# Decoding attention on one Trainium2 core: K and V of two sequences in one transfer each, and outputs gathered into token rows

## The chip, the cores and the metric

The kernel runs on one core of a Trainium2 chip. The metric is the device time of one execution in microseconds (us), the median of three runs. Engines are named as in the profile: PE multiplies matrices (PEld loads its weights), DVE, ACT and POOL work on vectors, SP here only issues DMAs. Sixteen DMA engines move data between HBM and the on-chip memory SBUF; PE writes its sums into the accumulator memory PSUM.

## What is computed

Eight sequences (B) bring four new tokens each (Sq). There are 32 query heads and 8 heads of K and V, so four query heads (rep) share one K and V; each head has 128 elements and the cache 2048 positions. All data are bf16.

```python
q = (x @ wq).reshape(B, Sq, Hq, Dh).transpose(0, 2, 1, 3)
k = jnp.repeat(k_cache, rep, axis=1)
v = jnp.repeat(v_cache, rep, axis=1)
scores = jnp.einsum("bhqd,bhkd->bhqk", q, k) * (Dh ** -0.5)
p = softmax(scores, axis=-1)
o = jnp.einsum("bhqk,bhkd->bhqd", p, v)
out = o.transpose(0, 2, 1, 3).reshape(B, Sq, Hq * Dh) @ wo
```

K and V are 33.5 MB each, wq and wo 4.2 MB each, x 32 KB: 75.5 MB in all, read once.

## The kernel before

The work is cut into eight units (NU). Unit u is a group of four K/V heads (G) and a pair of sequences (NB = 2); units 0 to 3 have the first group (gg = 0), units 4 to 7 the second. The 128 partitions hold four heads times 32 stretches of 64 positions (C), so one sequence's K of a unit is 2 MiB, 16 KB in a row on each partition.

**Loads.** All loads are issued on SP's queue into `ring`, eight slots of 2 MiB (L65, L67). `loads` (L118 to L123) lists them in order: K of unit 0, first sequence; x; wq in two halves; K of unit 0, second sequence; K of unit 1; then V of unit u and K of unit u + 2 in turn; last V in four pieces of 1 MiB (`load_last_v`) and wo (`load_wo`), its first half (for gg = 0) in rows of 4 KB, its second half in five pieces. `issue(done)` (L125) issues as many as the ring has slots for, once before the units and once at the end of each unit's pass (L368); a load into a slot that is still read waits on SP, and the loads behind it with it.

**One pass of the unit loop (L341).** For each of four tiles t of 16 positions: `turn` transposes the tile of K on DVE, once for either sequence (kt, six buffers); `scores` multiplies it with the queries on PE, eight matmuls into `s_ps`. In unit 7 the turns of the first sequence stand, like those of all units but 0, each ahead of the second's. `top` takes the maxima on DVE in two halves, `exps` the exponentials on ACT with their sums, `weights` transposes the result on DVE (pt) and copies it into `p_bd`, four block rows for each half h: three on ACT, one on POOL. `norm` makes the reciprocal of the sums on DVE. Then, one unit behind, `values(u-1)` multiplies with V on PE, 32 matmuls for each half, and `scaled` multiplies the result with the reciprocal on ACT into `o_sb`.

**Outputs.** The result of a unit has rows (head, sequence, query head, token), and a row computed both sequences' V; only the column block of its own sequence counts. Two units behind, `by_heads` (L280) gathers the right blocks by two matmuls with a permutation `perm`, and `to_rows` (L287) copies them (o_r) and transposes them on DVE into `oP`, once per unit. `project` (L298) multiplies `oP` with wo on PE into `out_ps`, 64 matmuls of 256 columns in all, after the last unit's values. The order at the end (L369 to L376): half of the first group's projection, `by_heads` and `to_rows` of unit 7, the other half, and the second group's projection as the pieces of wo land. Then one copy on ACT and two DMAs out.

The order on each engine is the order of the calls (`manual_schedule`, L63); waits between engines come from the data.

Of the kernel before, what the change touches and what calls it, by code (L numbers as in the profile page):

```python
# [17 lines left out]
def kernel(  # L18
# [31 lines left out]
    DH = D // 2  # L50
    scale = float(Dh) ** -0.5
# [19 lines left out]
    perm = const.tile([128, NB, 128], BF16, name="perm")  # L71
# [4 lines left out]
    oP = [const.tile([128, G, 4, NP, NB * Sq], BF16, name=f"oP{i}") for i in range(NG)]  # L76
# [11 lines left out]
    def load_kv(kind, u, b):  # L88
        gg, bp = units[u]
        src = (k_cache if kind == "k" else v_cache)[NB * bp + b, G * gg : G * gg + G]  # L90
        nc.sync.dma_start(  # L91
            ring[:, take((kind, u, b)), :], src.rearrange("g (s c) d -> (g s) (c d)", c=C)
        )

    def load_last_v(u):
        gg, bp = units[u]
        slots = [take(("v", u, b)) for b in range(NB)]
        for h in range(2):
            for b in range(NB):
                src = v_cache[NB * bp + b, G * gg : G * gg + G]  # L100
                nc.sync.dma_start(
                    ring[:, slots[b], h * CH * Dh : (h + 1) * CH * Dh],
                    src.rearrange("g (s c) d -> (g s) (c d)", c=C)[:, h * CH * Dh : (h + 1) * CH * Dh],
                )

    def load_wq(h):
        rows = wq.rearrange("(p r) n -> p (r n)", r=R)
        n = C * Dh
        nc.sync.dma_start(ring[:, take(("wq", h)), :], rows[:, h * n : (h + 1) * n])  # L109

    def load_wo(gg, cuts):
        slot = take(("wo", gg))
        rows = wo[gg * G * 512 : (gg + 1) * G * 512, :].rearrange("(k p r) j -> p k (r j)", k=G, r=4)
        to = ring[:, slot, :].rearrange("p (k n) -> p k n", k=G)
        for g0, g1, r0, r1 in cuts:
            nc.sync.dma_start(to[:, g0:g1, r0 * D : r1 * D], rows[:, g0:g1, r0 * D : r1 * D])

    loads = [("k", 0, 0), ("x",), ("wq", 0), ("wq", 1), ("k", 0, 1), ("k", 1, 0), ("k", 1, 1)]  # L118
    for u in range(NU):
        if u + 2 < NU:  # L120
            loads += [("v", u, 0), ("v", u, 1), ("k", u + 2, 0), ("k", u + 2, 1)]
    loads += [("v", NU - 2, 0), ("v", NU - 2, 1), ("vlast", NU - 1), ("wo", 0), ("wo", 1)]
    loads.reverse()  # L123

    def issue(done):  # L125

        while loads:
            what = loads[-1]
            if what[0] != "x" and n_loads[0] + (what[0] == "vlast") >= done + NS:
                return  # L130
            loads.pop()
            if what[0] in "kv":
                load_kv(*what)
            elif what[0] == "x":
                nc.sync.dma_start(x_sb[:, :], x.flatten_outer_dims())  # L135
            elif what[0] == "wq":
                load_wq(what[1])
            elif what[0] == "vlast":
                load_last_v(what[1])
            elif what[1] == 0:  # L140
                load_wo(0, [(0, 4, 0, 4)])
            else:
                load_wo(1, [(0, 1, 0, 4), (1, 2, 0, 4), (2, 3, 0, 4), (3, 4, 0, 2), (3, 4, 2, 4)])

    issue(0)
# [7 lines left out]
    by_row = ident[:, :].rearrange("k (g b r s) -> k b r g s", g=G, b=NB, r=rep)  # L153
    for b in range(NB):
        nc.gpsimd.tensor_copy(
            out=perm[:, b, :].rearrange("k (r g b s) -> k b r g s", r=rep, g=G, b=NB)[:, b],
            in_=by_row[:, b],
        )
# [3 lines left out]
    def turn(u, b, t):  # L162

        kt = ktpool.tile([128, CT, J, S, 2], BF16, tag="kt", name="kt")
        n = CT * Dh
        nc.vector.transpose(  # L166
            out=kt[:, :, :, :, :].rearrange("w c j s e -> w (c j s e)").bitcast(FP32),
            in_=ring[:, slot_of["k", u, b], t * n : (t + 1) * n].bitcast(FP32),
        )
        kts[u, b, t] = kt  # L170
# [28 lines left out]
    def top(u, h):  # L199
        if h == 0:  # L200
            stats[u] = [small.tile([128, n], FP32, tag=f"stat{i}", name=f"stat{i}") for i, n in enumerate((2, 1, 2, 1))]
        nc.vector.tensor_reduce(  # L202
            out=stats[u][0][:, h : h + 1],
            in_=s_ps[:, 2 * h : 2 * h + 2, :].rearrange("q t n -> q (t n)"),
            axis=AX,
            op=ALU.max,
            negate=True,
        )
# [26 lines left out]
    def weights(u, h):  # L235
        pt = small.tile([128, CH // 2, 32, 2], BF16, tag="pt", name="pt")
        nc.vector.transpose(  # L237
            out=pt[:, :, :, :].rearrange("s c q e -> s (c q e)").bitcast(FP32),
            in_=ps[u, h][:, :, :, :].rearrange("q c s e -> q (c s e)").bitcast(FP32),
        )  # L240
        pb = pbs[u, h] = p_bd[(2 * u + h) % 4]
        for g in range(G):
            rows = slice(g * 32, (g + 1) * 32)
            copy = nc.gpsimd.tensor_copy if g == G - 1 else nc.scalar.copy
            copy(out=pb[rows, :, g, :, :], in_=pt[rows, :, :, :])  # L245

    def norm(u):
        nc.vector.tensor_tensor(
            out=stats[u][3][:, :], in0=stats[u][2][:, 0:1], in1=stats[u][2][:, 1:2], op=ALU.add
        )  # L250
        nc.vector.reciprocal(stats[u][3][:, :], stats[u][3][:, :])
# [3 lines left out]
    def values(u, h):  # L255
        if h == 0:
            o_pss[u] = psum_o.tile([128, NB, Dh], FP32, tag="o", name="o_ps")
        a, b = (slot_of["v", u, i] for i in range(NB))
        v = (ring[:, a : b + 1 : b - a, :] if b > a else ring[:, a : (b - 1 if b else None) : b - a, :])
        v = v.rearrange("p b (c d) -> p b c d", d=Dh)  # L260
        for i in range(CH):
            nc.tensor.matmul(  # L262
                o_pss[u][:, :, :],
                lhsT=pbs[u, h][:, i // 2, :, :, i % 2].rearrange("s g q -> s (g q)"),
                rhs=v[:, :, h * CH + i, :],
                start=(h == 0 and i == 0),
                stop=(h == 1 and i == CH - 1),
            )
# [11 lines left out]
    def by_heads(u):  # L280
        o_pm = o_pms[u] = psum_m.tile([128, Dh], FP32, tag="m", name="o_pm")
        for b in range(NB):
            nc.tensor.matmul(  # L283
                o_pm[:, :], lhsT=perm[:, b, :], rhs=o_sbs[u][:, b, :], start=(b == 0), stop=(b == NB - 1)
            )

    def to_rows(u):  # L287
        gg, bp = units[u]
        o_r = small.tile([128, 4, 32], BF16, tag="o_r", name="o_r")
        nc.vector.tensor_copy(  # L290
            out=o_r[:, :, :], in_=o_pms[u][:, :].rearrange("q (d r) -> q r d", r=4)
        )
        nc.vector.transpose(
            out=oP[gg][:, :, :, bp, :].rearrange("d g r t -> d r g t"),
            in_=o_r[:, :, :].rearrange("q r d -> q (r d)"),
        )

    def project(gg, g, r0, n):  # L298
        w = ring[:, slot_of["wo", gg], :].rearrange("p (k r j) -> p k r j", k=G, r=4)
        for r in range(r0, r0 + n):  # L300
            for half in range(2):
                nc.tensor.matmul(  # L302
                    out_ps[half * T : (half + 1) * T, :],
                    lhsT=oP[gg][:, g, r, :, :].rearrange("d p t -> d (p t)"),
                    rhs=w[:, g, r, half * DH : (half + 1) * DH],
                    start=(gg == 0 and g == 0 and r == 0),
                    stop=(gg == NG - 1 and g == G - 1 and r == 3),
# [10 lines left out]
    for gg in range(NG):  # L318
        psq = psum_o.tile([128, rep * Dh], FP32, tag="o", name="psq")
        for r in range(R):  # L320
            w = ring[:, slot_of["wq", r // 2], :].rearrange("p (r n) -> p r n", r=2)[:, r % 2, :]
# [19 lines left out]
    for u in range(NU + 1):  # L341
        if u < NU:
            for t in range(NT):
# [3 lines left out]
                scores(u, t)  # L347
            if u >= 2:
                by_heads(u - 2)
# [4 lines left out]
            if u >= 2:  # L354
                to_rows(u - 2)
# [5 lines left out]
        if u >= 1:  # L361
            values(u - 1, 0)
            if u == NU:
                by_heads(u - 2)
                to_rows(u - 2)
# [46 lines left out]
```

## Time and profile before

| | us |
|---|---|
| runs (median of 3) | 186.34 (186.31 to 186.52) |
| the profiled execution | 186.44 |
| its span, first to last instruction | 184.3 |
| PE busy | 136.6 (74%) |
| DVE busy | 117.3 (64%) |
| ACT busy | 78.2 (42%) |
| POOL busy | 36.2 (20%) |

The mean granted PE clock is 0.953. The core read 75.53 MB from HBM. Busy shares are means over the whole span; which engine sets the end is read from the chain of waits, which follows back from the last instruction what released each step. A row of the timeline gives start, duration, engine, line, operation, output<-inputs, count, and in brackets the idle time before it with what ended it. A row of a windows view gives, behind the window and its length, busy time and count of PE, PEld, DVE, ACT and POOL, then the granted clock, the share of the DMA engines and GB/s. A DMA summary row gives packets, bytes and the rate in its window.

### The profile page before, as it was taken

How to read it: one execution, taken by the hardware profiler on the slowest of the kernel's cores; microseconds unless marked ns; L12 is line 12 of the kernel's file. 1: busy time of each engine (PE TensorE's matmuls, PEld its weight loads, DVE VectorE, ACT ScalarE, POOL GpSimd, SP SyncE). 2: the span in 40 equal slices, each digit the busy share in tenths (PEclk: the TensorE clock that was granted, in tenths of full speed). 3: DMA queues.
4: the chain of work that ended last, by engine and by line, in shares of the span. 5: the costliest groups of instructions: out<-in, count | busy, mean ns of one | idle time of the engine just before them, and what ended most of it. 6: DMA issues, size and time to landing. Idle time of an engine off the chain costs nothing.

```text
span 184.3 us, 2298 instructions
## 1 busy us (share of the span) xinstructions
PE 136.6 (74%) x884; PEld 81.5 (44%) x884; DVE 117.3 (64%) x147; ACT 78.2 (42%) x93; POOL 36.2 (20%) x92
## 2 busy tenths in 40 slices
PE   0001799039997998989759994989498949997992
PEld 0000233013683376338523771368135823486880
DVE  6680290689649976977488666976497549661110
ACT  2000200494079219905950298019900891059410
POOL 8500420080025005200800061005200210003000
PEclk9999999957999999999987999999979996999999
DMA  5999999999999999999999999999999999999980
GB/s 192 430 430 434 437 423 437 427 430 430 427 437 430 425 434 420 439 430 430 427 427 434 427 443 427 423 430 427 444 427 430 430 420 441 414 430 409 421 344 11
DMA packets 6586, 75.71 MB, mean 411 GB/s; under 512 B 720, under 2 KB 816, under 8 KB 1968
## 3 DMA queue, kind: packets, MB, share of 16 engines
q1 hardware_dynamic: 6528, 75.55, 96.6%
q8 instruction: 7, 0.11, 0.2%
q10 hardware_dynamic: 48, 0.02, 0.0%
q14 instruction: 3, 0.02, 0.0%
HBM read 75.53 MB, written 0.03 MB: 410 GB/s over the span
## 4 chain that ended last, share of the span: by engine, by line
DMA 68%; DVE 12%; PE 9%; issue 4%; ACT 3%; POOL 1%; SPq 1%; ACTq 0%; DVEq 0%; POOLq 0%
DMA ring<-in_k_cache_dram 43%; DMA ring<-in_v_cache_dram 17%; PE s_ps L189 9%; DVE kt L166 8%; DMA ring<-in_wo_dram 8%; DVE stat L202 3%; ACT p_sb L223 2%; POOL p_bd L245 1%; DVE pt L237 1%; SPq L109 1%; DVE stat L210 0%; SPq L135 0%; PE out_ps L302 0%; SPq L91 0%; ACT out_sb L379 0%
## 5 line engine op out<-in xcount | busy, mean ns | idle before, releaser
L189 PE MATMUL s_ps<-kt,q_bd 128*128 128x512 bf16 x256 | 70.5, 420 | 23.9 <-DVE kt L166 10.3
L166 DVE STREAM_TRANSPOSE kt<-ring 128x1024 f32<-128x1024 f32 x64 | 73.5, 1210 | 11.9 <-DMA ring<-in_k_cache_dram 11.9
L262 PE MATMUL o_ps<-ring,p_bd 128*128 128x256 bf16 x512 | 57.3, 272 | 3.2 <-DMA ring<-in_v_cache_dram 2.0
L189 PEld LDWEIGHTS <-q_bd 128*128 128x128 bf16 x256 | 25.9, 103 | 67.5 <-issue 31.6
L262 PEld LDWEIGHTS <-p_bd 128*128 128x128 bf16 x512 | 49.8, 98 | 9.9 <-issue 4.1
L223 ACT ACTIVATE p_sb<-s_ps,stat 128x1024 bf16<-128x1024 f32 x16 | 22.0, 1402 | 75.5 <-DVE stat L210 75.5
L245 ACT COPY p_bd<-pt 32x1024 bf16<-32x1024 bf16 x48 | 49.9, 1040 | 0.5
L245 POOL COPY p_bd<-pt 32x1024 bf16<-32x1024 bf16 x16 | 16.6, 1038 | 115.7 <-DVE pt L237 113.2
L202 DVE TENSOR_REDUCE stat<-s_ps 128x1 f32<-128x1024 f32 x16 | 18.9, 1220 | 13.3 <-PE s_ps L189 13.3
L237 DVE STREAM_TRANSPOSE pt<-p_sb 128x512 f32<-128x512 f32 x16 | 11.4, 711 | 15.0 <-ACT p_sb L223 15.0
L178 POOL COPY q_bd<-qT 32x64 bf16<-32x64 bf16 x64 | 13.0, 229 | 15.4 <-DVE qT L334 13.6
L323 PE MATMUL psq<-ring,xT_sb 128*32 128x512 bf16 x32 | 3.8, 626 | 8.2 <-DMA ring<-in_wq_dram 8.2
L290 DVE CAST o_r<-o_pm 128x128 bf16<-128x128 f32 x8 | 2.3, 284 | 10.1 <-PE o_pm L283 10.1
L314 PE MATMUL xtp<-ident,x_sb 32*128 32x32 bf16 x4 | 0.3, 192 | 8.9 <-DMA x_sb<-in_x_dram 8.9
L149 DVE MEMSET p_bd<- 128x2048 uint32 x3 | 5.3, 1765 | 2.0 <-PEq L396 1.2
L334 DVE STREAM_TRANSPOSE qT<-q_sb 128x64 f32<-128x64 f32 x8 | 1.2, 212 | 7.9 <-ACT q_sb L330 7.9
L330 ACT CAST q_sb<-psq 128x512 bf16<-128x512 f32 x2 | 1.2, 585 | 11.2 <-PE psq L323 11.2
L323 PEld LDWEIGHTS <-xT_sb 128*32 128x32 bf16 x32 | 1.2, 129 | 10.0 <-issue 9.5
L274 ACT ACTIVATE o_sb<-o_ps,stat 128x256 bf16<-128x256 f32 x8 | 3.8, 474 | 4.1 <-issue 3.9
L302 PE MATMUL out_ps<-ring,oP 128*32 128x256 bf16 x64 | 4.1, 273 | 0.2 <-DMA ring<-in_wo_dram 0.2
L314 PEld LDWEIGHTS <-x_sb 32*128 32x128 bf16 x4 | 0.2, 114 | 8.9 <-DMA x_sb<-in_x_dram 8.9
L302 PEld LDWEIGHTS <-oP 128*32 128x32 bf16 x64 | 3.0, 96 | 1.1 <-issue 0.6
(20 smaller groups left out, 21.9 us busy)
## 6 DMA issues: line engine op xcount, KB each, us to landing
ring<-in_k_cache_dram SPq DMA_DIRECT2D x16, 2048.0 KB, 27.1
ring<-in_v_cache_dram SPq DMA_DIRECT2D x14, 2048.0 KB, 30.1
ring<-in_wq_dram SPq DMA_DIRECT2D x2, 2048.0 KB, 14.1
ring<-in_v_cache_dram SPq DMA_DIRECT2D x4, 1024.0 KB, 29.4
ring<-in_wo_dram SPq DMA_DIRECT2D x1, 2048.0 KB, 26.9
ring<-in_wo_dram SPq DMA_DIRECT2D x3, 512.0 KB, 22.1
ring<-in_wo_dram SPq DMA_DIRECT2D x2, 256.0 KB, 15.7
x_sb<-in_x_dram SPq DMA_DIRECT2D x1, 32.0 KB, 7.7
```

Source lines behind the costliest of these rows:

```text
L149: nc.vector.memset(t[:, :, :, :, :], 0.0)
L166: nc.vector.transpose(out=kt[:, :, :, :, :].rearrange("w c j s e -> w (c j s e)").bitcast(FP32), in_=ring[:, slot_of["k", u, b], t * n : ( ...
L178: nc.gpsimd.tensor_copy(out=qb[rows, b, :, g, b, :].rearrange("w (j e) q -> w j e q", e=2), in_=qT[rows, gg, :, NB * bp + b, :, :, :].rear ...
L189: nc.tensor.matmul(s_ps[:, t, :], lhsT=q_bd[u % 2][:, b, 2 * j + e, :, :, :].rearrange("w g b q -> w (g b q)"), rhs=kts[u, b, t][:, :, j, ...
L202: nc.vector.tensor_reduce(out=stats[u][0][:, h : h + 1], in_=s_ps[:, 2 * h : 2 * h + 2, :].rearrange("q t n -> q (t n)"), axis=AX, op=ALU.max,
L223: nc.scalar.activation(out=p_sb[:, :, :, :].rearrange("q c s e -> q c e s"), in_=s_ps[:, 2 * h : 2 * h + 2, :].rearrange("q t (c e s) -> q ...
L237: nc.vector.transpose(out=pt[:, :, :, :].rearrange("s c q e -> s (c q e)").bitcast(FP32), in_=ps[u, h][:, :, :, :].rearrange("q c s e -> q ...
L245: copy(out=pb[rows, :, g, :, :], in_=pt[rows, :, :, :])
L262: nc.tensor.matmul(o_pss[u][:, :, :], lhsT=pbs[u, h][:, i // 2, :, :, i % 2].rearrange("s g q -> s (g q)"), rhs=v[:, :, h * CH + i, :], st ...
L274: nc.scalar.activation(out=o_sb[:, :, :], in_=o_pss[u][:, :, :], func=COPY, scale=stats[u][3][:, :])
L302: nc.tensor.matmul(out_ps[half * T : (half + 1) * T, :], lhsT=oP[gg][:, g, r, :, :].rearrange("d p t -> d (p t)"), rhs=w[:, g, r, half * D ...
L323: nc.tensor.matmul(psq[g * T : (g + 1) * T, :], lhsT=xT_sb[:, r, :], rhs=w[:, (gg * G + g) * rep * Dh : (gg * G + g + 1) * rep * Dh], star ...
```

## The change

- **Ring and loads.** Four slots of 4 MiB instead of eight of 2 MiB. K of a unit is one transfer for both sequences, and so is V; a partition gets two rows of 16 KB, which lie 4 MiB apart in HBM. K of unit 0 stays in two transfers, with x between them and the whole of wq (one transfer) ahead of the second. The last V comes in two halves of positions, each for both sequences. `issue` is called with 2 + 2u.
- **wo.** A partition holds 16 rows of wo in a row (16 KB), and not four rows in each of four blocks. The first half is one transfer as before; the second half is cut at rows 8, 12 and 14.
- **Outputs.** `norm` multiplies the reciprocal with a mask `of_b` that is 1 for the row's own sequence. `scaled` makes one sequence's part on ACT; `joined` adds the other's on DVE, after the sixth turn of the pass two units on (L373), and for units 6 and 7 after unit 7's weights. `by_tokens` uses four matmuls with shifted windows of `perm`, which place a unit's rows among 32 token rows of each head; four units of a group add up in one PSUM tile. `to_rows` then runs once a group: one copy of 512 columns, one transposition of 512 columns that reads with steps of 16 elements.
- **Unit 7's weights.** Two of the four copies of each half go to DVE, one stays on ACT, one on POOL.
- **The end.** Half of the first group's projection, `by_tokens` and `to_rows`, the other half, and the second group's projection.

The core of the diff; the setup of `perm` and `of_b` on POOL and DVE is left out:

```diff
-    NS = 8
+    NS = 4
...
-    ring = ring_pool.tile([128, NS, C * Dh], BF16, name="ring")
+    ring = ring_pool.tile([128, NS, NB, C * Dh], BF16, name="ring")
...
+    def load_kv(kind, u, parts):
+
         gg, bp = units[u]
+        slot = take((kind, u))
+        src = (k_cache if kind == "k" else v_cache)[NB * bp : NB * bp + NB, G * gg : G * gg + G]
+        rows = src.rearrange("b g (s c) d -> (g s) b (c d)", c=C)
+        n = C * Dh
+        for b0, b1, h0, h1 in parts:
+            h0, h1 = int(h0 * n), int(h1 * n)
+            yield nc.sync.dma_start(ring[:, slot, b0:b1, h0:h1], rows[:, b0:b1, h0:h1])
+
+    def load_wq():
+        slot = take("wq")
         nc.sync.dma_start(
+            ring[:, slot, :, :].rearrange("p b n -> p (b n)"), wq.rearrange("(p r) n -> p (r n)", r=R)
+        )
+
+    def load_wo():
+        slot = take("wo")
+        for gg, cuts in ((0, (0, RW)), (1, (0, 8, 12, 14, 16))):
+            rows = wo[gg * G * 512 : (gg + 1) * G * 512, :].rearrange("(p r) j -> p (r j)", r=RW)
+            for r0, r1 in zip(cuts, cuts[1:]):
+                nc.sync.dma_start(ring[:, slot, gg, r0 * D : r1 * D], rows[:, r0 * D : r1 * D])
...
             copy = nc.gpsimd.tensor_copy if g == G - 1 else nc.scalar.copy
+            if u == NU - 1 and g < 2:
+                copy = nc.vector.tensor_copy
             copy(out=pb[rows, :, g, :, :], in_=pt[rows, :, :, :])
...
+        nc.vector.tensor_scalar_mul(stats[u][3][:, :], of_b[:, :], stats[u][4][:, :])
...
         nc.scalar.activation(
-            out=o_sb[:, :, :], in_=o_pss[u][:, :, :], func=COPY, scale=stats[u][3][:, :]
+            out=o_sb[:, 0, :], in_=o_pss[u][:, 0, :], func=COPY, scale=stats[u][3][:, 0:1]
+        )
+
+    def joined(u):
+        o_sb = o_sbs[u]
+        nc.vector.scalar_tensor_tensor(
+            out=o_sb[:, 1, :],
+            in0=o_pss[u][:, 1, :],
+            scalar=stats[u][3][:, 1:2],
+            in1=o_sb[:, 0, :],
+            op0=ALU.mult,
+            op1=ALU.add,
         )
...
+    def by_tokens(u):
+        gg, bp = units[u]
+        if bp == 0:
+            o_pms[gg] = psum_m.tile([128, rep, Dh], FP32, tag="m", name="o_pm")
+        w = 32 - NB * Sq - bp * NB * Sq
+        for r in range(rep):
             nc.tensor.matmul(
+                o_pms[gg][:, r, :],
+                lhsT=perm[:, r, w : w + 128],
+                rhs=o_sbs[u][:, 1, :],
+                start=(bp == 0 and r == 0),
+                stop=(bp == NP - 1),
+                skip_group_check=True,
             )
 
+    def to_rows(gg):
+        o_r = q_sb[:, 0, :, :, :, :].rearrange("k r j w e -> k (r j w e)")
+        nc.vector.tensor_copy(out=o_r, in_=o_pms[gg][:, :, :].rearrange("k h d -> k (h d)"))
         nc.vector.transpose(
+            out=oP[gg][:, :, :], in_=o_r.rearrange("k (h g r) -> k r h g", h=rep, r=RW)
+        )
...
                 scores(u, t)
+                if t == NT - 2 and u >= 2:
+                    joined(u - 2)
...
         if u >= 1:
             values(u - 1, 0)
             if u == NU:
-                by_heads(u - 2)
-                to_rows(u - 2)
+                joined(u - 2)
+                by_tokens(u - 2)
             values(u - 1, 1)
             scaled(u - 1)
-        issue(4 + 4 * u)
-    project(0, 0, 0, 4)
-    project(0, 1, 0, 4)
-    by_heads(NU - 1)
-    to_rows(NU - 1)
-    project(0, 2, 0, 4)
-    project(0, 3, 0, 4)
-    for g in range(G):
-        project(1, g, 0, 4)
+            if u == NU:
+                joined(u - 1)
+        issue(2 + 2 * u)
+    project(0, 0, RW // 2)
+    by_tokens(NU - 1)
+    to_rows(NG - 1)
+    project(0, RW // 2, RW)
+    project(1, 0, RW)
```

More of the change, by code (lines that the diff above doesn't have):

```diff
@@ L106, in load_wq @@
[L106 to L116, printed above, removed]
@@ L119 @@
     for u in range(NU):
+        loads.append(("v", u))
         if u + 2 < NU:
-            loads += [("v", u, 0), ("v", u, 1), ("k", u + 2, 0), ("k", u + 2, 1)]
-    loads += [("v", NU - 2, 0), ("v", NU - 2, 1), ("vlast", NU - 1), ("wo", 0), ("wo", 1)]
+            loads.append(("k", u + 2))
+    loads.append("wo")
     loads.reverse()
     def issue(done):
[L127 to L134, printed above, removed]
-                nc.sync.dma_start(x_sb[:, :], x.flatten_outer_dims())
[L136 to L141, printed above, removed]
-            else:
-                load_wo(1, [(0, 1, 0, 4), (1, 2, 0, 4), (2, 3, 0, 4), (3, 4, 0, 2), (3, 4, 2, 4)])
+        while loads and n_loads[0] < done + NS:
+            what = loads.pop()
+            if what == "k0":
+                first = load_kv("k", 0, [(0, 1, 0, 1), (1, 2, 0, 1)])
+                next(first)
+                nc.sync.dma_start(x_sb[:, :], x.flatten_outer_dims())
+                held.append(first)
+            elif what == "wq":
+                load_wq()
+                for _ in held.pop():
+                    pass
+            elif what == "wo":
+                load_wo()
+            else:
+                last = what == ("v", NU - 1)
+                for _ in load_kv(*what, [(0, NB, 0, 0.5), (0, NB, 0.5, 1)] if last else whole):
+                    pass
@@ L200, in top @@
         if h == 0:
[L201 removed]
+            stats[u] = [small.tile([128, n], FP32, tag=f"stat{i}", name=f"stat{i}") for i, n in enumerate((2, 1, 2, 2, 1))]
         nc.vector.tensor_reduce(
@@ L276, in scaled @@
         )
     o_pms = {}
[L280 to L284, printed above, removed]
-            )
[L287 to L291, printed above, removed]
-        )
[L293 to L296, printed above, removed]
@@ L303, in project @@
                     out_ps[half * T : (half + 1) * T, :],
[L304 to L307, printed above, removed]
+                    lhsT=oP[gg][:, r, :],
+                    rhs=w[:, r, half * DH : (half + 1) * DH],
+                    start=(gg == 0 and r == 0),
+                    stop=(gg == NG - 1 and r == RW - 1),
                 )
@@ L353 @@
             top(u, 1)
-            if u >= 2:
-                to_rows(u - 2)
+            if u >= 2 and units[u - 2][1] == NP - 1:
+                to_rows(units[u - 2][0])
             for h in range(2):
```

62 lines of the change are left out of this document (30 added, 32 removed).

## The prediction

> **What bounds the kernel now.** I read the slices first, then the chain of waits in order of time, then the DMA rates, and last the timeline of the final unit.
>
> ```profile
> span 184.3 us, 2298 instructions
> DMA  5999999999999999999999999999999999999980
> 64.71 27.93 DMA ring<-in_k_cache_dram
> 100.70 30.80 DMA ring<-in_k_cache_dram
> 135.05 30.52 DMA ring<-in_v_cache_dram
> 165.59 14.89 DMA ring<-in_wo_dram
> 180.52 0.41 PE out_ps L302 x4
> 180.96 0.36 ACT out_sb L379
> ```
>
> The DMA engines are 90% busy or more in 37 slices of 40, and the chain (start, duration) runs from one landing to the next: 92.64, 131.50, 165.57, 180.48. From 92.64 to 131.50 eight 2 MiB transfers land (K4 second half to K6 second half), 4.858 us each. After the last piece of wo there are only four matmuls, a copy and the output, 184.3 - 180.5 = 3.8 us, which the change leaves alone. So the end moves if the last landing moves, or if the compute behind the last K (unit 7) stops fitting under the last loads. Bytes stay the same; what can change is the time lost between bytes.
>
> ```profile
> DMA packets 1337, 19.41 MB, mean 431 GB/s; under 512 B 152, under 2 KB 152, under 8 KB 152
> DMA packets 288, 1.18 MB, mean 421 GB/s; under 512 B 0, under 2 KB 0, under 8 KB 288
> q10 hardware_dynamic: 48, 0.02, 21.2%
> ring<-in_k_cache_dram SPq DMA_DIRECT2D x16, 2048.0 KB, 27.1
> ring<-in_v_cache_dram SPq DMA_DIRECT2D x14, 2048.0 KB, 30.1
> ring<-in_wo_dram SPq DMA_DIRECT2D x1, 2048.0 KB, 26.9
> 148.57 0.38 SPq L116 DMA_DIRECT2D ring<-in_wo_dram  x1
> ```
>
> The first row is the stretch 100 to 145 us (16 KB packets), the second 170.2 to 173 (wo's 4 KB packets alone), the third the output on ACT's queue from 182.2 to 182.5. The last rows say how early loads are issued: K lands 27.1 us after its issue, of which its own 2 MiB takes 4.9.
>
> **The change, part by part.**
>
> *Packets.* A packet is one contiguous row on one of 16 engines. wo's first half was 512 packets of 4 KB, 32 an engine, and becomes 16 KB rows, 8 an engine: 24 fewer. The second half goes from 24 of 4 KB and 16 of 2 KB to 8 of 8 KB, 8 of 4 KB and 16 of 2 KB: 8 fewer. Price: 16 x 4096 B at 421 GB/s is 0.1557 us, 16 x 16384 B at 431 is 0.6082; four small ones cost 0.6227, so three extra packets cost 0.0145, 0.005 us each. 32 x 0.005 = **0.16 us saved**.
>
> *Completions.* Loads fall from 43 to 25 (K 16 to 9, V 18 to 9, wq 2 to 1, wo 6 to 5, x 1): 18 fewer, each with one completion packet an engine. No row shows one alone. The q10 row bounds it: 48 packets, 32 of 512 B and 16 completions, took 21.2% of 16 engines for 0.3 us, 1.02 us, 0.021 each on average; the lower bound is 0. I take the middle, 0.010: 18 x 0.010 = **0.18 us saved** (0 to 0.38). A saving per transfer cannot be larger by much: the eight transfers above took 4.858 us, and 8 packets an engine at 0.6082 are already 4.866.
>
> *K in one transfer.* Its two halves landed 4.9 us apart, and one transposition of the next unit could run ahead. Now all eight wait for both halves:
>
> ```profile
> 150.97 8.00 DVE L166 STREAM_TRANSPOSE kt<-ring 128x1024 f32<-128x1024 f32 x7 [2.46 <-DMA ring<-in_k_cache_dram]
> 152.27 8.15 PE L189 MATMUL s_ps<-kt,q_bd 128*128 128x512 bf16 x28 [2.58 <-DVE kt L166]
> 160.46 2.36 DVE L202 TENSOR_REDUCE stat<-s_ps 128x1 f32<-128x1024 f32 x2 [1.49 <-PE s_ps L189]
> 164.74 0.71 DVE L237 STREAM_TRANSPOSE pt<-p_sb 128x512 f32<-128x512 f32 x1 [1.13 <-ACT p_sb L223]
> 165.58 1.04 POOL L245 COPY p_bd<-pt 32x1024 bf16<-32x1024 bf16 x1 [17.29 <-DVE pt L237]
> 165.86 6.31 ACT L245 COPY p_bd<-pt 32x1024 bf16<-32x1024 bf16 x6
> 169.10 3.65 PE L262 MATMUL o_ps<-ring,p_bd 128*128 128x256 bf16 x32 [1.21 <-issue]
> ```
>
> In unit 7 eight transpositions of 8.00/7 = 1.14 us, plus the joining operation put after the sixth (0.29, from the 128-element cast below), end at 150.97 + 9.14 + 0.29 = 160.40; K lands about 0.12 earlier (14 completions at most 0.14), so 160.28, against 158.97. PE was the later one before (152.27 + 8.15 = 160.42, part of it at a lower clock); now the last transposition is, and four more matmuls (8.15/28 = 0.29 each at worst) end at 161.3 to 161.45. **Scores end 0.9 to 1.0 us later.** Queued behind on DVE are the maxima, so ACT's exps and everything after. In units 1 to 6 the same 1.1 us costs nothing: K's slot is free that much later, but the next K is issued 22 us before its first byte is due. At the start q has to wait for all of wq:
>
> ```profile
> 13.63 1.04 PE L323 MATMUL psq<-ring,xT_sb 128*32 128x512 bf16 x8 [4.43 <-DMA ring<-in_wq_dram]
> 18.47 2.75 PE L323 MATMUL psq<-ring,xT_sb 128*32 128x512 bf16 x24 [3.79 <-DMA ring<-in_wq_dram]
> ```
>
> The first eight matmuls join the others behind 18.47, so q is up to 1 us later. Unit 0's turns of K0's second half may follow, and with them the issue of K2 on SP and of V1 queued behind it. But the ring takes 16 MiB before that issue, 39 us of transfers at 431 GB/s; an issue that comes at 30 instead of 28 us leaves no gap.
>
> *Weights of unit 7.* 160.42 to ACT's first copy at 165.86 is 5.44, so now 166.8. ACT does one copy (6.31/6 = 1.05) instead of three before the first half is ready: 167.85 against 169.01. DVE takes two. No row shows DVE copying 1024 bf16; bounds are 0.29 (a 128-element cast) and 1.14 (the 1024-element transposition). The nearest row is pt's transposition, the same 2 KB a partition in and out: 0.71. At that they end at 165.45 + 0.9 + 1.42 = 167.77, beside ACT's. So PE starts on the values at 167.9: **1.2 us earlier** than 169.10.
>
> *Turning once, at the end.*
>
> ```profile
> 176.42 1.05 PE L302 MATMUL out_ps<-ring,oP 128*32 128x256 bf16 x16
> 177.41 0.28 PE L283 MATMUL o_pm<-o_sb,perm 128*128 128x128 bf16 x2
> 177.73 0.29 DVE L290 CAST o_r<-o_pm 128x128 bf16<-128x128 f32 x1 [4.05 <-PE o_pm L283]
> 178.06 0.31 DVE L293 STREAM_TRANSPOSE oP<-o_r 128x128 bf16<-128x128 bf16 x1
> 177.62 2.69 PE L302 MATMUL out_ps<-ring,oP 128*32 128x256 bf16 x44
> ```
>
> From 169.10 the values take to 176.42; from 167.9, with two more gathering matmuls (0.11), they end at 175.3. PE then needs wo's first half: 148.57 + 26.9 = 175.5 before, about 175.2 now, no wait. Sixteen projections take 0.99 (176.42 to 177.41). Under them lie unit 7's scaling on ACT, now half as wide, and the joining on DVE, 0.3 to 0.5 each. Four gathering matmuls end at 176.7. The cast has 512 elements instead of 128: between the casts' 0.29 and the reductions' 1.18 by length, 0.69. The turn has 512: 0.71 by pt's row. The second projection can start at 176.75 + 0.69 + 0.71 + 0.1 = 178.25. Its first 28 matmuls (2.69/44 = 0.061) end at 179.95, or a little before; the last piece of wo lands at 180.48 - 0.34 = 180.14. **Cover left: about 0.2 to 0.3 us.** If it is gone, each further 0.1 us of lateness costs 0.1.
>
> The turn reads bf16 elements 16 apart, 32 B, which no row shows. The cast's 16 B steps in the accumulator cost nothing that its 0.29 shows, so I take no penalty; bounds 0 and 0.71 (twice as long). [...] No row of this profile reads SBUF on DVE with such steps.
>
> **Sum.** 0.16 + 0.18 = 0.34 us off the last landing, nothing added if the cover holds. The profiled execution took 186.44, 2.1 around its span of 184.3: 186.10. The median of the runs is 186.34, 0.10 lower: **186.0 us**, own range 185.8 to 186.2 (completions 0 to 0.38).
>
> **Rivals.**
>
> *The tail is late (slower).* One mechanism: the chain scores, weights, cast, turn of unit 7 passes wo's last landing. It decides from 0.25 us of lateness, and gives a slower kernel from 0.25 + 0.34 = 0.6. Strided turn at twice, 0.71, with DVE copies at 1.14 each, (1.14 - 0.71) x 2 = 0.86: 1.57 late, less 0.6 is +0.97, 187.3; the turn alone, +0.1; both halfway, +0.2; turn whole and half the copies, 0.71 + 0.43 - 0.6 = +0.54, 186.9. For: the cover is thin and two of its prices are unseen. Against: DVE's order and ACT's relief give back 1.2 us first.
>
> *Nothing is saved.* If completions and packet starts overlap other packets' data, or the thin cover gives them back, 186.3. For: 4.858 us for eight packets whose price came out at 4.866 leaves no visible completion. Against: the 421 against 431 GB/s.
>
> *The engines' skew (faster).*
>
> ```profile
> q8 instruction: 7, 0.11, 0.2%
> 178.00:178.80 0.80, 0.80 (x20) 0.72 (x16) 0.33 (x2) 0.00 (x0) 0.00 (x0) 1.00 0.78 294
> 178.80:179.60 0.80, 0.80 (x19) 0.73 (x17) 0.00 (x0) 0.00 (x0) 0.00 (x0) 1.00 0.45 172
> 179.60:180.40 0.80, 0.71 (x12) 0.40 (x7) 0.00 (x0) 0.00 (x0) 0.00 (x0) 1.00 0.11 41
> ```
>
> The DMA share (last but one column) falls from 0.78 to 0.11 over the last 2.4 us: the 16 engines don't end together, and the slowest sets the end. Seven instruction blocks of 16 KB ride on single engines, 0.6 us or more each. With 32 more PE instructions they fall elsewhere; if the slowest engine is spared one, 0.6 less: 185.4. As likely a neighbour is hit instead, so it is seldom worth more than 0.2.
>
> *Streaming slows.* One transfer alternates between two sequences 4 MiB apart. The 67.1 MB of K and V take 156 us at 431 GB/s, so each per cent costs 1.6 us; 3% gives 191. For: nothing shown. Against: the 16 engines are spread over several packets already (next to last view), so one sequence's end and the next one's start were read side by side before, at 431 GB/s. [...]
>
> **How the numbers follow.** Forecast 0.50, nothing saved 0.17, late tail 0.17, skew 0.12, slower streaming 0.04. A measurement of this kernel tells 0.2% (0.37 us) from no change, so the border is 185.97, just below the forecast: of its 0.50, 0.20 lies below and 0.30 above. Faster: 0.20 + 0.12 = 0.32. Same: 0.30 + 0.17 + 0.03 of the late tail = 0.50. Slower: 0.14 + 0.04 = 0.18. The range runs from 185.6 to 186.9, leaving out the worst of the late tail, streaming and the largest skew.
>
> **What would show it.** Right: transfers of 4 MiB about 9.7 us apart; wo's first half at 431 rather than 421 GB/s; the last landing near 180.1; PE idle before the last four projections, ended by wo; scores of unit 7 ending near 161.3, values starting near 167.9, the one turn at 0.7. Wrong: a last wait of PE on DVE's oP (late tail), a turn of 1.2 or more, landings further apart than 9.75, or a chain that leaves the DMA rows before the last unit.

## The result, and the profile after

The changed kernel takes 186.12 us (median of 22 runs) against 186.52 for the kernel before in 22 runs beside it; the ratio is 0.998 (0.9971 to 0.9988). Every kernel of this case, the old one too, has executions 4 to 15 us longer, in one profile of the changed kernel at 382 GB/s over the span against 411 (and one kernel of the study had a single one of 353.61 us, not explained); the ratios, the table and the profiles shown leave them out, and the profile after is for that reason one of the same kernel run again.

The table sets beside each kernel's time its mean span (first to last instruction) and what the time holds outside the span. It is the key to the result. The three groups of the study ran on three chips; the kernel before ran beside each:

| kernel | runs | median us | mean span | outside the span |
|---|---|---|---|---|
| before, beside the three groups of kernels below | 9, 11, 12 | 186.27, 186.25, 186.30 | 184.1, 184.2, 184.1 | 2.13, 2.15, 2.16 |
| after | 13 | 185.92 | 184.2 | 1.81 |
| after, again (two runs of the study) | 1 and 4 | 185.8 and 185.8 | 184.0 and 184.3 | 1.80 and 1.77 |
| new loads, old outputs (two runs) | 7 and 5 | 185.69 and 185.59 | 183.7 and 183.7 | 1.96 and 1.97 |
| after, transfers split again | 7 | 185.65 | 183.9 | 1.82 |
| after, cast by rows | 7 | 185.52 | 183.7 | 1.85 |
| after, copies of unit 7 left on ACT | 2 | 187.97 | 185.8 | 2.22 |
| before, idle instructions on PE, DVE and POOL | 2 | 185.90 | 184.1 | 1.80 |
| before, idle instructions on DVE alone | 8 | 185.99 | 184.3 | 1.80 |
| before, idle instructions on PE and POOL alone | 1 | 186.13 | 184.0 | 2.13 |
| after, cast by rows, last K and last wo split | 2 | 185.69 | 183.9 | 1.84 |

By the ratio the time went down by 0.37 us. The span did not: 184.2 stands against 184.1 to 184.2, and 0.32 to 0.35 us of the gain lie outside it. Inside the span something was won and given back. The page of the changed kernel (186.44 became 185.83 in the profiled execution):

```profile
span 184.1 us, 2321 instructions
PE 134.9 (73%) x900; PEld 82.0 (45%) x900; DVE 127.9 (69%) x157; ACT 73.4 (40%) x89; POOL 37.8 (21%) x98
DMA  6999999999999999999999999999999999999980
```

The DMA slices are as full as before, and DVE has ten instructions more and 10.6 us more work. The chain of waits of the same execution, in order of time (start, duration, what; here and below its pieces called `issue`, 0.02 to 0.14 us each, are mostly left out), no longer ends in wo:

```profile
83.76 27.71 DMA ring<-in_k_cache_dram
...
120.91 29.77 DMA ring<-in_k_cache_dram
150.70 1.26 DVE kt L175
152.09 9.08 PE s_ps L198 x32
161.40 10.48 PE o_ps L272 x96
172.10 3.49 PE o_ps L272 x32
175.59 0.98 PE out_ps L327 x16
176.57 0.34 PE o_pm L307 x4
176.94 0.70 DVE q_sb L318
177.67 1.11 DVE oP L319
178.82 1.94 PE out_ps L327 x32
180.78 0.37 ACT out_sb L405
```

Before, the chain went V of the last units, wo, four matmuls. Now it leaves the DMA rows at 150.68 (120.91 + 29.77) with unit 7's K, and from there on every step is compute: scores, values, projection, gathering, cast, turn, projection. The timeline of that end (start, duration, engine, line, output<-inputs, in brackets the idle time before and its releaser):

```profile
161.21 2.36 DVE L211 TENSOR_REDUCE stat<-s_ps 128x1 f32<-128x1024 f32 x2 [1.12 <-PE s_ps L198]
...
166.24 1.60 DVE L256 COPY p_bd<-pt 32x1024 bf16<-32x1024 bf16 x2
166.34 1.23 POOL L256 COPY p_bd<-pt 32x1024 bf16<-32x1024 bf16 x1 [17.03 <-DVE pt L246]
...
166.75 1.04 ACT L256 COPY p_bd<-pt 32x1024 bf16<-32x1024 bf16 x1
...
176.94 0.69 DVE L318 CAST q_sb<-o_pm 128x512 bf16<-128x512 f32 x1 [0.51 <-PE o_pm L307]
177.67 1.10 DVE L319 STREAM_TRANSPOSE oP<-q_sb 128x512 bf16<-128x512 bf16 x1
178.82 1.92 PE L327 MATMUL out_ps<-ring,oP 128*32 128x256 bf16 x32 [0.93 <-DVE oP L319]
```

The last row is the verdict: PE stands idle for 0.93 us before the second projection, and what ends the wait is DVE's `oP`, not wo. The last piece of wo had been issued at 155.07 and lands 24.9 us later, at 179.98, half a microsecond before the 180.48 of the kernel before; the windows view (window, length, busy time and count of PE, PEld, DVE, ACT, POOL, then clock, DMA share, GB/s) shows the loads thinning out earlier:

```profile
178.00:178.80 0.80, 0.00 (x0) 0.00 (x0) 0.76 (x1) 0.00 (x0) 0.00 (x0) 1.00 0.57 220
178.80:179.60 0.80, 0.78 (x16) 0.72 (x18) 0.00 (x0) 0.00 (x0) 0.00 (x0) 1.00 0.29 110
179.60:180.40 0.80, 0.80 (x20) 0.74 (x16) 0.00 (x0) 0.00 (x0) 0.00 (x0) 1.00 0.01 3
```

In the last window the DMA share was 0.11 and is 0.01, while PE, at the full clock, is busy throughout with projections that it could have begun in the first window. PE ends at 180.76, 0.78 after the last landing; before, it ended 0.45 after it.

### The profile page after: what moved, and what is told of

Same layout as the page of the kernel before. It is cut to its first block, busy times and chain, and to the rows that moved or that the text cites. A ratio compares the mean times of both kernels' runs of the same rounds, so it can differ in the third digit from the quotient of the medians.

```text
span 198.4 us, 2321 instructions
## 1 busy us (share of the span) xinstructions
PE 138.5 (70%) x900; PEld 83.3 (42%) x900; DVE 128.1 (65%) x157; ACT 73.3 (37%) x89; POOL 37.6 (19%) x98
## 4 chain that ended last, share of the span: by engine, by line
DMA 60%; DVE 21%; PE 13%; issue 2%; ACT 1%; SPq 1%; DVEq 0%; ACTq 0%
DMA ring<-in_k_cache_dram 60%; DVE kt L175 17%; PE o_ps L272 7%; PE s_ps L198 5%; PE out_ps L327 1%; ACT p_sb L232 1%; DVE stat L211 1%; DVE oP L319 1%; DVE stat L263 0%; PE o_pm L307 0%; DVE pt L246 0%; DVE q_sb L318 0%; DVE o_sb L290 0%; SPq L131 0%; SPq L104 0%
## 5 line engine op out<-in xcount | busy, mean ns | idle before, releaser
L198 PE MATMUL s_ps<-kt,q_bd 128*128 128x512 bf16 x256 | 72.5, 440 | 35.0 <-DVE kt L175 22.3
L198 PEld LDWEIGHTS <-q_bd 128*128 128x128 bf16 x256 | 27.0, 108 | 79.6 <-issue 43.6
L256 ACT COPY p_bd<-pt 32x1024 bf16<-32x1024 bf16 x44 | 45.8, 1040 | 1.3 <-DVE pt L246 0.8
L263 DVE TENSOR_SCALAR stat<-of_b,stat 128x2 f32<-128x2 f32 x8 | 5.9, 733 | 0.3
L290 DVE SCALAR_TENSOR_TENSOR o_sb<-o_ps,stat,o_sb 128x128 bf16<-128x128 f32 x8 | 2.5, 317 | 5.0 <-ACT o_sb L284 5.0
L284 ACT ACTIVATE o_sb<-o_ps,stat 128x128 bf16<-128x128 f32 x8 | 2.9, 367 | 5.8 <-PE o_ps L272 5.6
```

The lines of the kernel that those rows point to most:

```text
L198: nc.tensor.matmul(s_ps[:, t, :], lhsT=q_bd[u % 2][:, b, 2 * j + e, :, :, :].rearrange("w g b q -> w (g b q)"), rhs=kts[u, b, t][:, :, j, ...
L263: nc.vector.tensor_scalar_mul(stats[u][3][:, :], of_b[:, :], stats[u][4][:, :])
```

## The experiments

**One part of the change at a time.** The first group is the changed kernel again and three variants: the loads without the outputs, the outputs with the transfers split, and the turn with its steps moved into the cast.

The changed kernel again:

> The changed kernel once more, for its profile and its time. My forecast (fewer packets and completions move the last landing forward, the tail is covered): about 0.3 us less than before, last landing of wo near 180.1, PE's last wait on wo. The late tail (unit 7's cast and turn end after wo): the last wait of PE is on oP, last landing at least 0.3 earlier than the start of the last projections. Nothing saved: last landing within 0.1 of 180.5.

It took 185.8 us with a span of 184.0, in one run: that agrees with the 13 others and says no more. A second run gave the profile above:

> The changed kernel once more for an undisturbed profile. New theory (PE sets the tail: after the scores of unit 7 it still has 64 matmuls of unit 6's values, 7.0 us, so the values of unit 7 start near 168.4 and not at 167.9; with a turn of 1.1 us the second projection starts near 178.85 and ends near 180.8, 0.1 before the kernel before): PE's last wait is on oP, about 0.9 us, and wo's last landing is near 180.0, 0.4 or more before that end. My forecast of a covered tail: PE's last wait is on wo, end near 180.5.

185.77, 185.80, 185.83 and 186.99, ratio 0.9994 (0.9945 to 1.0042). With so few runs, and the last so far from the others, the interval is too wide to tell anything; the profile was what it was for.

The loads without the outputs. The old kernel gets the four slots of 4 MiB, K, V and wq in whole transfers, and DVE's copies in unit 7; wo keeps its rows of 4 KB and each unit is turned by itself:

```diff
-    NS = 8
+    NS = 4
...
-    loads = [("k", 0, 0), ("x",), ("wq", 0), ("wq", 1), ("k", 0, 1), ("k", 1, 0), ("k", 1, 1)]
+    whole = [(0, NB, 0, 1)]
+    loads = ["k0", "wq", ("k", 1)]
...
+            if u == NU - 1 and g < 2:
+                copy = nc.vector.tensor_copy
```

> The kernel before with the 4 MiB ring and transfers for K, V and wq and with DVE copies in unit 7, but with its own outputs and wo in 4 KB rows. My forecast: only the completions are saved, 17 x 0.010 = 0.17 us less than before, last landing near 180.3. If completions cost nothing: same as before within 0.1. If 4 MiB transfers stream slower: landings further than 9.75 us apart and a longer time.

> The loads alone once more for an undisturbed profile. If the slowest DMA engine's lag makes most of the difference: last landing near 180.0 although wo still moves in 4 KB rows, and the DMA share in the last us higher than before. If completions make it: landings of 4 MiB transfers 0.02 or more closer than two of 2 MiB (below 9.69), and the same end of the DMA share as before.

Ratios 0.9968 (0.9955 to 0.9981) and 0.9959 (0.9945 to 0.9973); the span is 183.7, 0.46 and 0.51 less than that of the kernel before beside them. This kernel's chain of waits still ends in wo:

```profile
165.48 14.74 DMA ring<-in_wo_dram
180.27 0.41 PE out_ps L301 x4
180.70 0.36 ACT out_sb L378
```

wo lands at 180.22, 0.26 before its landing in the profile of before, and the outputs, turned unit by unit, keep up. But the old loads are seen to do the same: in the old kernel with idle instructions, further down, wo lands at 180.23 and the last copy starts at 180.70 too. The spans of these two executions, 183.7 and 184.1, differ only behind that copy, where no load of K, V or wo and no matmul is left. So it is not shown that the new loads by themselves let the last load land earlier; why the stretch behind the copy is 0.4 us shorter here stays open.

The transfers split. K of both sequences goes in two transfers again, V and its last halves too; all else is as changed:

```diff
-    whole = [(0, NB, 0, 1)]
+    whole = [(0, 1, 0, 1), (1, 2, 0, 1)]
+    halves = [(b, b + 1, h, h + 0.5) for h in (0, 0.5) for b in range(NB)]
```

> The changed kernel, but K and V in one transfer per sequence again (16 transfers more, the last V in four), all else as changed. My forecast: 16 x 0.010 = 0.16 us slower than the changed kernel at the last landing, the first turn of the next unit runs ahead again, so scores of unit 7 end about 0.9 us earlier after K's landing and any wait of PE on oP disappears. Late tail: faster than the changed kernel, by what PE waited on oP less 0.16. Completions cost nothing and the tail is covered: same as the changed kernel.

185.65 us, ratio 0.9971 (0.9956 to 0.9985). Sixteen transfers more cost next to nothing: the last landing is at 180.04 in its trace, 0.07 later than with whole transfers, that is 0.004 us each. And one transposition can run ahead again: seven of the eight are left behind K's landing, five of them in the first row of its timeline. Yet the chain of waits, below it, shows where that head start goes:

```profile
150.74 5.75 DVE L176 STREAM_TRANSPOSE kt<-ring 128x1024 f32<-128x1024 f32 x5 [1.36 <-DMA ring<-in_k_cache_dram]
...
160.12 2.36 DVE L212 TENSOR_REDUCE stat<-s_ps 128x1 f32<-128x1024 f32 x2 [1.12 <-PE s_ps L199]
```

```profile
148.29 26.84 DMA ring<-in_wo_dram
175.17 1.05 PE out_ps L328 x16
176.22 0.34 PE o_pm L308 x4
176.59 0.70 DVE q_sb L319
177.31 1.11 DVE oP L320
178.47 2.03 PE out_ps L328 x32
```

The scores of unit 7 end 1.1 us earlier (the maxima start at 160.12, not 161.21), but the first projection then waits for wo's first half, which lands at 175.13. The gathering is queued behind it on PE, so cast and turn come only 0.35 us earlier and the second projection starts at 178.47 in place of 178.82.

The turn without steps. The cast, which reads the accumulator, now reads with steps of 16 elements (64 B) and writes in the order in which the turn needs it; the turn reads in a row:

```diff
-        nc.vector.tensor_copy(out=o_r, in_=o_pms[gg][:, :, :].rearrange("k h d -> k (h d)"))
+        nc.vector.tensor_copy(
+            out=o_r.rearrange("k (r h g) -> k r h g", r=RW, h=rep),
+            in_=o_pms[gg][:, :, :].rearrange("k h (g r) -> k r h g", r=RW),
+        )
...
-            out=oP[gg][:, :, :], in_=o_r.rearrange("k (h g r) -> k r h g", h=rep, r=RW)
+            out=oP[gg][:, :, :].rearrange("d r t -> d (r t)"), in_=o_r
```

> The changed kernel, but the cast of to_rows writes its 512 elements in the order of the turn (reading PSUM with steps of 16 elements), and the turn reads them in a row. Turn reading steps of 32 B costs extra: turn 0.7 us instead of 1.1, cast 0.7 if PSUM steps cost nothing, up to 1.4 if they do. Late tail: 0.4 us faster than the changed kernel at most, by what PE waited on oP. My forecast of a covered tail: same as the changed kernel within 0.1.

185.52 us, ratio 0.9963 (0.9947 to 0.9979), the lowest median of the study; the interval overlaps that of the changed kernel, so what the edit does is read from the trace. Its timeline:

```profile
177.01 0.69 DVE L318 CAST q_sb<-o_pm 128x512 bf16<-128x512 f32 x1 [0.51 <-PE o_pm L307]
177.73 0.71 DVE L322 STREAM_TRANSPOSE oP<-q_sb 128x512 bf16<-128x512 bf16 x1
...
178.50 1.92 PE L330 MATMUL out_ps<-ring,oP 128*32 128x256 bf16 x32 [0.55 <-DVE oP L322]
180.47 0.36 ACT L408 CAST out_sb<-out_ps 64x256 bf16<-64x256 f32 x1 [4.35 <-PE out_ps L330]
```

The turn falls from 1.10 to 0.71 us and the cast does not rise from its 0.69, so the steps cost 0.39 us in SBUF and nothing that shows in the accumulator. The final copy on ACT moves from 180.78 to 180.47, and the mean span from 184.2 to 183.7. The last landing, read from this kernel's trace, is 179.98 as in the changed kernel, and the last four matmuls behind it would end no earlier than 180.43; PE ends at 180.44. PE still waits for `oP` before the second projection, but the tail is now just at the loads' bound.

**ACT's copies in unit 7.** Is DVE's help needed, which the prediction counted as 1.2 us? The two lines that move copies to DVE are taken out:

```diff
-            if u == NU - 1 and g < 2:
-                copy = nc.vector.tensor_copy
```

> The changed kernel without DVE copies in unit 7 (three on ACT again). New theory (PE is busy with unit 6's values until 168.4, then waits for the weights): the first half of the weights is ready near 169.9, values of unit 7 start 1.5 us later than in the changed kernel and the end moves by the same 1.5: about 187.4. Covered tail: 0.35 less than that, near 187. If ACT's copies were never on the path: same as the changed kernel.

187.92 and 188.01 us, ratio 1.0084 (1.0055 to 1.0114). The span grows from 184.2 to 185.75, by 1.6. By the rows of the changed kernel, three copies on ACT from 166.75 end the first half's weights at 169.87; PE, which is free for them at 168.4, starts 1.5 us late, and the second half's three copies, done at 173.0, are then in time. The kernel's own trace, in which the whole of unit 7 comes 6.1 us later, has this wait in its last row: unit 6's 64 matmuls end at 174.50, and unit 7's first 32 start 1.47 later.

```profile
167.35 7.15 PE L270 MATMUL o_ps<-ring,p_bd 128*128 128x256 bf16 x64
...
175.97 3.65 PE L270 MATMUL o_ps<-ring,p_bd 128*128 128x256 bf16 x32 [1.47 <-issue]
```

So most of the 1.6 is this one delay: the tail has no cover left, and lateness costs its full price. The other 0.4 of the longer time lies outside the span (2.22 against 1.81).

**The time outside the span.** The changed kernel has 10 more instructions on DVE, 16 more on PE and 6 more on POOL. To see what that alone does, the old kernel got as many that serve nothing: 10 clears of 8 columns on DVE and 6 on POOL after the set-up of `perm`, and the four matmuls that turn x run five times.

```diff
+    for i in range(10):
+        nc.vector.memset(pad[:, 8 * i : 8 * i + 8], 0.0)
+    for i in range(6):
+        nc.gpsimd.memset(pad[:, 96 + 8 * i : 104 + 8 * i], 0.0)
...
-    for r in range(R):
+    for r in [r for r in range(R) for _ in range(5)]:
```

> The kernel before with 16 more matmuls on PE (the transposition of x repeated), 10 small memsets on DVE and 6 on POOL at the start, where these engines are idle: the changed kernel's instruction counts, the same work otherwise. The time outside the span is 2.12 us before and 1.81 changed. If the length of the programs sets it: 1.8 here and the median 0.3 lower than before. If not: 2.1, and the same median.

185.89 and 185.90 us, 0.35 less than without them. The page's counts and its chain of waits:

```profile
PE 137.7 (75%) x900; PEld 82.5 (45%) x900; DVE 117.4 (64%) x157; ACT 78.3 (43%) x93; POOL 36.4 (20%) x98
```

```profile
165.37 14.86 DMA ring<-in_wo_dram
180.23 0.04 issue
180.27 0.41 PE out_ps L307 x4
180.70 0.36 ACT out_sb L384
```

Two things are seen. With the old loads wo lands at 180.23, not 180.48: a landing can move by 0.25 us without any change to a load; whether by the program's length or from one execution to the next is not shown. And the span is that of the kernel before, 184.1, while the time outside it fell from 2.15 to 1.80. The next two kernels keep only DVE's clears, or only PE's and POOL's part:

```diff
+    for i in range(10):
+        nc.vector.memset(pad[:, 8 * i : 8 * i + 8], 0.0)
```

> The kernel before with 10 small memsets on DVE at the start, nothing else. If DVE's instruction count sets the time outside the span (183 to 189 instructions went with 2.0 to 2.2 us, 193 with 1.8): 1.8 us outside the span and a median near 185.95. If PE's or POOL's does: 2.1 and 186.3.

> The kernel before with the 16 more matmuls on PE and the 6 memsets on POOL, without the memsets on DVE. The other way round: 2.1 us outside the span and 186.3 if DVE's count sets it, 1.8 and 185.95 if PE's or POOL's does.

DVE's clears alone: 185.99 us, ratio 0.9988 (0.9978 to 0.9998), 1.80 outside the span in the mean of eight runs (1.74 to 1.87), where the 12 runs of the kernel before beside it had 2.11 to 2.25. PE's and POOL's part alone: 186.13 us, 2.13 of it outside the span. That is one run, but it lies in the one range and far from the other. So ten instructions on DVE that do nothing take 0.35 us off the time outside the span. The whole time falls by less, 0.22 us by the ratio and 0.31 by the medians, as the spans of these eight runs are 0.13 longer in the mean.

**The best version.** The cast by rows, with K of unit 7 in two transfers, so that one transposition runs ahead, and the last piece of wo cut once more:

```diff
-        for gg, cuts in ((0, (0, RW)), (1, (0, 8, 12, 14, 16))):
+        for gg, cuts in ((0, (0, RW)), (1, (0, 8, 12, 14, 15, 16))):
...
+                if what == ("k", NU - 1):
+                    parts = [(b, b + 1, 0, 1) for b in range(NB)]
```

> The row cast of the fourth run, with the last K again in one transfer per sequence and wo's last piece cut at row 15 as well. New theory (with the short turn PE's tail and wo's landing end together): scores of unit 7 end 0.9 us earlier after K's landing, PE's last wait is on wo, two matmuls instead of four after the last landing save about 0.1: 185.4 to 185.5, against 185.55 for the row cast alone. Rival (the tail still sets the end): PE's last wait on oP and no difference, or slower by the extra transfers.

185.76 and 185.61 us, a span of 183.9: no better than the cast by rows alone. Its chain of waits:

```profile
177.33 0.72 DVE oP L325
178.10 2.07 PE out_ps L333 x30
180.18 0.30 PE out_ps L333 x2
180.50 0.37 ACT out_sb L411
```

The second projection starts 0.40 us earlier, at 178.10, and the copy is at 180.50, as late as the 180.47 without these edits. The last piece of wo lands at 180.14 in this trace, 0.16 later than in the cast by rows, and the last two matmuls wait for it. Once the tail fits, the last landing sets the end.

## Why the prediction was right, and where it was not

The forecast was 186.0 us, a gain of 0.34; the median is 0.12 above it (that of the table's 13 runs 0.08 below), the gain 0.37 by the ratio. The number held, but by luck, and not by the sum that gave it: the sum's terms lie in the span, and the span gave nothing; the gain came from a term that the sum held fixed. Point by point:

**Packets and completions: the landing.** "0.16 + 0.18 = 0.34 us off the last landing" forecast 180.14; it came at 179.98. Against the old loads in a program of equal length (180.23) that is 0.25, against the profile of before (180.48) 0.50. That profile has a span of 184.3, where the kernel's mean is 184.1 to 184.2, so the smaller figure is the nearer one. The direction is right. The landings in the traces, one execution each, say something of the two terms:

- Packets. From the landing of unit 6's V to that of the last piece of wo, the three kernels with rows of 4 KB (before, padded, new loads alone) take 19.76 to 19.80 us. With long rows it is 19.60 (changed), 19.55 (cast by rows), and 19.66 and 19.69 with more transfers. That is 0.07 to 0.25 less, where 0.16 was forecast: the term fits. wo's first half moved at 424 GB/s (170.2 to 173 us), not at the 431 that the prediction named as a sign.
- Completions. 15 of the 18 transfers saved lie ahead of the landing of unit 6's V. It came at 160.38 in the changed kernel, 160.39 with the transfers split again, 160.42 with the new loads alone and 160.46 in the padded old kernel (160.70 in the profile of before). So 0.08 is seen against a program of equal length, where 0.15 was forecast, and 16 transfers more made the last landing 0.07 later, 0.004 each and not 0.010. With a spread of 0.25 between programs the size of a completion is not settled. The prediction's own comparison, 4.858 us for a transfer against 4.866 for its packets alone, had left nothing for one; the middle of the bounds was a choice.

**K in one transfer.** Scores were to end 0.9 to 1.0 us later, at 161.3 to 161.45. The maxima wait for them until 161.21: right within 0.1. That it costs nothing in the earlier units also held: the stream ran at the same rate, below.

**Weights of unit 7.** "PE starts on the values at 167.9" failed. The copies did come as forecast: DVE's two took 1.60 us together (1.42 forecast), ending at 167.84. But PE was not free. Behind the scores its queue holds the four gathering matmuls, from 161.17, and the 64 matmuls of unit 6's values; the row of 96 matmuls starts at 161.40 in the chain and takes 0.109 us each, so 64 of them end at 168.4. PE is the one that sets this point, with no idle time at all in 161.40 to 171.88. The prediction read the 1.21 us of idle time before the values in the old timeline as a gap that the copies alone decide, and forgot that scores ending 0.9 us later push unit 6's values too. The values end at 175.59 (forecast 175.3), the gathering at 176.91 (176.7): 0.2 us late.

**The turn.** "I take no penalty" failed. Cast: 0.69 forecast, 0.69 measured. Turn: 0.71 forecast, 1.10 measured, 0.39 more, inside the bounds of 0 to 0.71. The run with the cast by rows shows that it is the steps: the same turn, reading in a row, took 0.71. It took 1.5 times as long with the steps (1.10 against 0.71), where the upper bound was twice.

**The cover.** 0.22 of PE and 0.39 of the turn make 0.6 of lateness (178.82 against 178.25), where 0.25 were to spare. So the rival "the tail is late" came true, with a small size: PE ends at 180.76 instead of 180.43 (179.98 and the last four matmuls), which is the 0.3 that the cast by rows brings back. The prediction gave this rival 0.17 and the form it took, a turn halfway to its bound; it was the step "Cover left: about 0.2 to 0.3 us" that should have warned more. In the rival's own terms, a slower kernel needed 0.6 of lateness, and that is where the span came out: 184.2 against 184.1 to 184.2.

**The missing term.** Of the measured gain 0.32 to 0.35 us are time outside the span, from 2.13 to 2.16 down to 1.81. The prediction took the "2.1 around its span" as fixed. That ten idle instructions on DVE give the old kernel the same 0.35 is shown; by which way, is not.

**The other rivals.** Streaming does not slow. The DMA summary of 100 to 145 us in the changed kernel (packets, bytes, rate):

```profile
DMA packets 1259, 19.39 MB, mean 431 GB/s; under 512 B 75, under 2 KB 75, under 8 KB 75
```

The 431 GB/s are those of before, with half as many packets of under 2 KB. Two transfers of 4 MiB took 19.40 us from the landing at 131.28 to the one at 150.68 (9.70 each, as forecast), but 19.81 from 111.47 to 131.28. Of the 13 steps between the landings from 32.87 to 160.38, five are longer than the 9.75 that the prediction set as a sign of slower streaming. The mean is 9.81 all the same, and the kernel before has 9.82 for the same 4 MiB, so the sign was set too tight. So a second row 4 MiB away on the same partition costs nothing here. For "the engines' skew" there is a spread of 0.25 us between programs with equal loads, about what the prediction gave it; that the skew makes it is not shown, and the change shows no such sign of its own; the traces compared come from three chips. "Nothing is saved" is wrong for the time and, in the mean, right for the span.

## What to carry to other kernels

A transfer that ends earlier is worth only what the work queued behind it lets through: follow each engine's queue by itself, the matmuls of the unit before included, up to the last projection, before a cover of a few tenths is counted on. Where a layout needs an operand read with steps, put the steps into the pass that reads the accumulator, and let the transposition read in a row: here that is worth 0.39 us on the path. And where a gain is below half a per cent, look at the span and at the rest of the time apart: ten instructions that do nothing took as much off the time outside the span, 0.35 us, as the whole change did.

## What was not expected of the hardware

**DVE's multiply ends with POOL's copy.** DVE's copies of one shape in unit 7 and the small multiply in `norm` have two durations each (minimum, median and maximum in ns, first and last start, forms):

```profile
L256 POOL COPY p_bd<-pt x16: 1040/1041/1228, 37.2 to 168.7; 32x1024 bf16<-32x1024 bf16 x16
...
L256 DVE COPY p_bd<-pt x4: 416/795/1176, 166.2 to 169.1; 32x1024 bf16<-32x1024 bf16 x4
```

```profile
L263 DVE TENSOR_SCALAR stat<-of_b,stat x8: 228/890/925, 38.8 to 170.6; 128x2 f32<-128x2 f32 x8
```

The timeline shows what goes with the long ones:

```profile
148.26 1.04 POOL L256 COPY p_bd<-pt 32x1024 bf16<-32x1024 bf16 x1 [0.30 <-DVE stat L259]
148.41 0.92 DVE L263 TENSOR_SCALAR stat<-of_b,stat 128x2 f32<-128x2 f32 x1
...
170.63 0.23 DVE L263 TENSOR_SCALAR stat<-of_b,stat 128x2 f32<-128x2 f32 x1
```

A multiply of two columns takes 0.92 us when a POOL copy began 0.15 before it, and ends when that copy ends, at 149.3; with POOL idle it takes 0.23. The traces with the transfers split, with the cast by rows and of the best version show the same: the multiply that begins 0.14 us after a POOL copy takes 0.92 to 0.93 and ends within 0.03 of that copy's end, and the last one, with POOL idle, takes 0.23. Of the two copies on DVE in each half, one takes 0.416 and one 1.176, beside a POOL copy that takes 1.23 instead of 1.04. What lengthens them is not shown. The mean of DVE's two copies, 0.80, happened to be near the 0.71 that the prediction took. No kernel without the POOL copy was run, so its share in the tail is not measured.

**The time outside the span depends on the program.** It was 2.13 to 2.16 us (means) with 147 instructions on DVE (the kernel before), 1.77 to 1.85 with 157 (the changed kernel, the kernels derived from it, and the old one with ten clears), and with 151 (the new loads alone) it lay between 1.73 and 2.17 from run to run. The kernel with the copies left on ACT (153) had 2.22. So it does not follow the count step by step; whether it is the count at all stays open.

The span's own end varies as well: from the start of the last copy to the end of the span it is 3.4 us in the kernel before (180.96 to 184.3) and in the padded one (180.70 to 184.1), 3.3 in the changed kernel (180.78 to 184.1) and 3.0 with the new loads alone (180.70 to 183.7). The prediction took what follows the last piece of wo as fixed; these differences are as large as the gain it forecast, and no run shows what sets them.
